# Pairing the attention chunks of a fused attention and mixture-of-experts kernel on one Trainium2 core

## The chip, the cores and the metric

The kernel runs on one core of one Trainium2 chip. The metric is the device time of one execution in microseconds (us); the value compared is the median of several runs. Five engines work side by side: TensorE (PE in the profile, its weight loads PEld), VectorE (DVE), ScalarE (ACT), GpSimd (POOL) and SyncE (SP), whose queue issues most of the DMAs.

## The reference

```python
def _attn_ref(r, k, v, w, u):            # B, H, S, D = 4, 8, 768, 48
    for t in range(S):
        cur = np.einsum('bhd,bhe->bhde', u[None] * kt, vt)
        y[:, :, t] = np.einsum('bhd,bhde->bhe', rt, state + cur)
        state = w[None, :, :, None] * state + np.einsum('bhd,bhe->bhde', kt, vt)

def _moe_ref(x, w1, w2, w3, w_out):      # 3072 tokens, 384 -> 768 -> 384
    h = np.maximum(np.maximum(x @ w1, x @ w2), x @ w3)
    return h @ w_out

def _moe2_ref(x, w_gate, w_noise, noise, w1, w2):   # 8 experts, top 2, 384 -> 1024 -> 384
    ...
```

A linear attention with a decaying state makes the tokens x. A dense layer takes the maximum of three products and projects it back. A router then sends each token to two of eight experts and adds their weighted results.

## The kernel before

The first part (to about 395 us) handles the 3072 tokens as 8 **blocks** of 384 tokens. A block is 21 **units**: 18 dense units `u_step(b, f, j)` (one of the three products for 128 of the 768 features; in block 0 three products in full float32, later nine in the split form wH and wl) and 3 projection units `x2_step(b, j)`. A dense unit writes one of two rotating PSUM banks `u`; the unit two places later writes the same bank, so it must wait until the earlier one has been read. Of the three units of a feature group, the first is read by ACT (copy to `uw`), the second and the third by DVE (`uw` = max).

The attention is done in **chunks** of 128 tokens, three for each block, one block ahead of the dense layer; every 6 chunks the state starts afresh. For a chunk, PE makes the scores (`scores`, into the banks `sc`), which DVE masks into `A`; one slot later the values `A`·v and `Rp`·state (`ymm`, bank `y`) and the state's increment (bank `st`). DVE adds these to `x` and to the next state `St`. For chunks below `NPE` = 6, PE also makes the scaled keys and the bonus weights (`x2` bank, then ACT copies `K2` and eight `sv` pieces); later chunks load a token-major copy and let DVE do that.

The units in which PE turns to attention are written down by hand: `SLOTS` = units 2, 9 and 17 of each block; there PE makes the values of one chunk and the scores of the next, one after the other. I call this a **burst**. The rest of a chunk's preparation (`prep`) is a generator of which one instruction is issued per unit. Chunks must also be transposed (token to feature order) for the dense layer: chunks 0 to 5 and every third one after that on PE (`xtr`, three transposes at unit `XTR` = 19 for the third chunk of a block), the others by a **bounce**: SP writes `x` to DRAM, reads it back in four pieces, and DVE transposes 32 by 32 (`x_bounce`, `x_turn`, five units after the burst).

DVE's remaining time is handed out by `fill`: it has a budget `room` per unit, and spends it on converting the weights (`conv`, block 0), splitting them (`splits`, blocks 0 and 1) and the router of the block before (`rgen`). Engines take their instructions in the order in which the program issues them.

The second part (from about 395 us) runs the experts. Neither its code nor its order differs between the two versions.

Of the kernel before, what the change touches and what calls it, by code (L numbers as in the profile page):

```python
# [7 lines left out]
F32 = mybir.dt.float32  # L8
# [30 lines left out]
SLOTS = (2, 9, 17)  # L39
# [4 lines left out]
TABK = 12  # L44
# [152 lines left out]
def moe_kernel(ctx, tc, rT, kT, tm, wuT, wrow, urow, mw, wout, wgn, noise, ew1, ew2, out):  # L197
# [159 lines left out]
    def prep(g):  # L357

        r_, k_, t_, v_ = LD[g]
        a = A_[g] = Ctx()  # L360
        a.v = v_
        a.Pk = at.tile([DP, 4, 128], F32, name="Pk", bufs=2)
        a.Rp = at.tile([DP, 4, 128], F32, name="Rp", bufs=2)
        a.K2 = at.tile([128, 4 * DP + 8], F32, name="K2", bufs=2)
        a.sv = at.tile([128, DM], F32, name="sv", bufs=2)
        yield v.tensor_mul(a.Pk, k_, Tk)
        yield v.tensor_mul(a.Rp, r_, Tr)
        t1 = at.tile([128, 512], F32, name="t1", tag="t1")
        if g < NPE:

            t1 = t1[:DP].rearrange("p (a c) -> p a c", a=4)
            yield v.tensor_mul(t1, r_, k_)
            pk = bank("x2")
            for pr in range(4):
                for th in TH:
                    nc.tensor.matmul(pk[th, pr * DP:pr * DP + DP], a.Pk[:, pr, th], Dg[:DP, pr * DP:pr * DP + DP],
                                     start=True, stop=True)
            red = pk[:, 4 * DP:4 * DP + 8]
            for pr in range(4):
                for th in TH:  # L380
                    nc.tensor.matmul(red[th, 2 * pr:2 * pr + 2], t1[:, pr, th], wu[:, pr, 1:], start=True, stop=True)
            nc.scalar.activation(a.K2, pk[:, :4 * DP + 8], AF.Copy)
            if g > 3:
                yield
            yield
            for h in range(H):
                hs = slice(h * D, h * D + D)
                nc.scalar.activation(a.sv[:, hs], a.v[:, hs], AF.Copy, scale=a.K2[:, 4 * DP + h:4 * DP + h + 1])
            return
        else:  # L390
            t1 = t1[:, :DM]
            tr, tk = t_[:, :DM], t_[:, DM:DM + 4 * DP]
            red = at.tile([128, H, 1], F32, name="red")
            yield v.tensor_mul(t1.rearrange("p (a b d) -> p a b d", a=4, b=2),
                               tr.rearrange("p (a b d) -> p a b d", a=4, b=2), gap(tk))
            yield v.tensor_mul(a.K2[:, :4 * DP], tk, TAB["k"])
            yield v.tensor_mul(t1, t1, ub)
            yield v.tensor_reduce(red, hd(t1), axis=AX.X, op=OP.add)
            yield v.tensor_mul(hd(a.sv), hd(a.v), red.to_broadcast([128, H, D]))
# [1145 lines left out]
```

## Time and profile before

| | us |
|---|---|
| median of 3 runs | 854.38 (854.34 to 855.59) |
| the profiled execution | 854.07 |
| its span, first to last instruction | 852.3 |

| engine | busy, us | share of the span |
|---|---|---|
| PE | 835.5 | 98% |
| DVE | 525.1 | 62% |
| ACT | 282.1 | 33% |
| POOL | 142.6 | 17% |

The busy time of PE overlaps: consecutive matmuls are pipelined, so the distance from one start to the next, and not a matmul's own duration, is the pace. DVE's share is a mean over stages that differ.

### The profile page before, as it was taken

What the parts mean: (1) busy time and instruction counts of PE and PEld (TensorE: products, weight loads), DVE (VectorE), ACT (ScalarE), POOL (GpSimd) and SP (SyncE); (2) the same over time, 40 slices, a digit from 0 to 9 for tenths busy, and PEclk for the clock granted to TensorE, in tenths of its full rate; (3) what the DMA queues carried; (4) which work ended last, traced back from release to release, by engine and by line L of the source; (5) the groups of instructions that cost most, each with busy time, mean ns of one, the idle gap of its engine ahead of it and who ended that gap; (6) DMA issues with size and microseconds to landing.
All of it is one profiled execution on the core that took longest, in us unless ns stands there. A gap on an engine that the chain in (4) does not pass through costs nothing.

```text
span 852.3 us, 17123 instructions
## 1 busy us (share of the span) xinstructions
PE 835.5 (98%) x6672; PEld 775.5 (91%) x6672; DVE 525.1 (62%) x1389; ACT 282.1 (33%) x600; POOL 142.6 (17%) x124
## 2 busy tenths in 40 slices
PE   8999999999999999999999999999999999999995
PEld 6667999999999999999989999999999999999994
DVE  8998987768677676837546672664626446264320
ACT  6334422212221231223314552433524344243221
POOL 1000030110303030110223031220222203122121
PEclk9999999999999999999999999999999999999998
DMA  9991252635525161125129774672555726553222
GB/s 288 321 257 48 81 179 72 211 135 154 179 70 159 47 182 51 39 103 131 58 70 218 191 161 102 146 170 64 124 126 133 169 78 126 119 141 47 49 30 32
DMA packets 98957, 107.82 MB, mean 127 GB/s; under 512 B 55361, under 2 KB 81714, under 8 KB 98866
## 3 DMA queue, kind: packets, MB, share of 16 engines
q1 hardware_dynamic: 88002, 86.68, 36.5%
q0 software_dynamic: 10320, 19.10, 10.8%
q8 instruction: 54, 0.88, 0.4%
q10 hardware_dynamic: 544, 0.85, 0.4%
q14 instruction: 37, 0.30, 0.1%
HBM read 73.96 MB, written 33.01 MB: 126 GB/s over the span
## 4 chain that ended last, share of the span: by engine, by line
PE 86%; DVE 5%; issue 4%; DMA 2%; POOL 1%; ACT 1%; SPq 0%; ACTq 0%; POOLq 0%; DVEq 0%
PE b_u L619 8%; PE b_u L621 7%; PE b_u L620 7%; PE b_u L860 7%; PE b_u L859 7%; PE b_u L861 7%; PE b_u L617 3%; PE b_y L426 3%; PE b_sc L407 2%; PE b_y L431 1%; PE b_y L887 1%; PE b_y L888 1%; PE b_st L889 1%; PE b_x L887 1%; PE b_tx L889 1%
## 5 line engine op out<-in xcount | busy, mean ns | idle before, releaser
L871 DVE SCALAR_TENSOR_TENSOR ghL<-b_u,ghH 128x512 fp32r<-128x512 f32 (+5 forms) x120 | 70.0, 584 | 188.9 <-ACT ghH L870 188.8
L859 PE MATMUL b_u<-gxH,e1H 128*128 128x512 f32 (+5 forms) x384 | 132.9, 346 | 0.4 <-ACT gxH L826 0.4
L860 PE MATMUL b_u<-gxL,e1H 128*128 128x512 f32 (+5 forms) x384 | 132.1, 344 | 0.1
L861 PE MATMUL b_u<-gxH,e1L 128*128 128x512 f32 (+5 forms) x384 | 131.8, 343 | 0.0
L619 PE MATMUL b_u<-xHt,wH 128*128 128x384 f32 x378 | 130.8, 346 | 0.8 <-DVE uw L628 0.8
L621 PE MATMUL b_u<-xHt,wl 128*128 128x384 f32 x378 | 127.6, 337 | 0.0
L620 PE MATMUL b_u<-xLt,wH 128*128 128x384 f32 x378 | 127.1, 336 | 0.0
L704 POOL DMA_INDIRECT XS<-rows,ii x48 | 55.2, 1150 | 384.5 <-issue 192.3
L870 ACT ACTIVATE ghH<-b_u 128x512 fp32r<-128x512 f32 (+5 forms) x120 | 61.4, 511 | 158.1 <-PE b_u L861 152.3
L861 PEld LDWEIGHTS b_u<-gxH,e1L 128*128 128x128 f32 x384 | 72.1, 188 | 8.9
L859 PEld LDWEIGHTS b_u<-gxH,e1H 128*128 128x128 f32 x384 | 72.3, 188 | 6.8 <-ACT gxH L826 0.6
L860 PEld LDWEIGHTS b_u<-gxL,e1H 128*128 128x128 f32 x384 | 72.2, 188 | 6.2 <-DVE gxL L833 0.3
L619 PEld LDWEIGHTS b_u<-xHt,wH 128*128 128x128 f32 x378 | 71.0, 188 | 4.6 <-issue 2.9
L630 ACT ACTIVATE hHt<-uw 128x384 fp32r<-128x384 f32 x48 | 25.2, 525 | 149.9 <-DVE uw L628 146.6
L952 POOL DMA_INDIRECT out_dram<-ys,gix x34 | 53.1, 1561 | 126.8 <-ACT ys L983 106.6
L628 DVE TENSOR_TENSOR uw<-b_u,uw 128x384 f32<-128x384 f32 x96 | 53.2, 554 | 31.0 <-PE b_u L621 27.3
L620 PEld LDWEIGHTS b_u<-xLt,wH 128*128 128x128 f32 x378 | 71.4, 189 | 0.0
L621 PEld LDWEIGHTS b_u<-xHt,wl 128*128 128x128 f32 x378 | 70.8, 187 | 0.0
L952 POOL DMA_INDIRECT out_dram<-yrows,gix x20 | 30.6, 1529 | 189.6 <-ACT yrows L946 185.7
L826 ACT ACTIVATE gxH<-raw 128x512 fp32r<-128x512 f32 (+4 forms) x48 | 26.1, 543 | 79.4 <-DVE raw L825 77.1
L624 ACT ACTIVATE uw<-b_u 128x384 f32<-128x384 f32 x48 | 23.5, 489 | 42.1 <-PE b_u L621 37.2
L617 PE MATMUL b_u<-xHt,wl 128*128 128x384 f32 x96 | 32.8, 492 | 0.0
(299 smaller groups left out, 1762.9 us busy)
## 6 DMA issues: line engine op xcount, KB each, us to landing
est<-in_ew_dram SPq DMA_DIRECT2D x64, 384.0 KB, 4.1
ldt<-in_tm_dram SPq DMA_DIRECT2D x18, 416.0 KB, 5.2
raw<-XS SPq DMA_DIRECT2D x32, 192.0 KB, 4.2
wS<-in_w_dram SPq DMA_DIRECT2D x15, 384.0 KB, 7.2
ldr<-in_rT_dram SPq DMA_DIRECT2D x24, 224.0 KB, 5.6
ldk<-in_kT_dram SPq DMA_DIRECT2D x22, 224.0 KB, 5.6
out_dram<-zrow SPq DMA_DIRECT2D x8, 576.0 KB, 4.7
cols<-in_tm_dram SPq DMA_DIRECT2D x22, 192.0 KB, 6.0
```

What stands on the lines that cost most here:

```text
L617: nc.tensor.matmul(o, WF[3 * f + j][:, ks], xH[b][:, k, :], start=(k == 0), stop=(k == 2))
L619: nc.tensor.matmul(o, WH[j][:, f, ks], xH[b][:, k, :], start=(k == 0), stop=False)
L620: nc.tensor.matmul(o, WH[j][:, f, ks], xL[b][:, k, :], start=False, stop=False)
L621: nc.tensor.matmul(o, WL[3 * f + j][:, ks], xH[b][:, k, :], start=False, stop=(k == 2))
L628: v.tensor_tensor(w, o, w, op=OP.max)
L704: st = nc.gpsimd.indirect_dma_start(out=XS, out_offset=bass.IndirectOffsetOnAxis(ap=ii[:, 3 * k + j:3 * k + j + 1], axis=0), in_=rw[:, j, ...
L859: nc.tensor.matmul(u, a[:, k, fs], o.xH[:, k, :n], start=(k == 0), stop=False)
L860: nc.tensor.matmul(u, a[:, k, fs], o.xL[:, k, :n], start=False, stop=False)
L861: nc.tensor.matmul(u, b[:, k, fs], o.xH[:, k, :n], start=False, stop=(k == 2))
L870: nc.scalar.activation(hH[:, :n], u, AF.Relu)
L871: v.scalar_tensor_tensor(hL[:, :n], u, 0.0, f32(hH[:, :n]), op0=OP.max, op1=OP.subtract)
L952: st = nc.gpsimd.indirect_dma_start(out=out, out_offset=bass.IndirectOffsetOnAxis(ap=o.ix[:o.n[j], j, :], axis=0), in_=ys, in_offset=None, ...
```

## The change

- `BURSTS` replaces `SLOTS`: a table of 14 bursts in place of 21. Up to chunk 9 a burst has one chunk's values and one chunk's scores. The burst at block 2, unit 2 has the values of chunk 9 and the scores of 10 and 11; from there each has the values of two chunks and the scores of the next two. The seven pairs are 10 and 11, 12 and 13, up to 22 and 23.
- In a pair the first chunk's state increment comes first and its values after it, into the bank `x2`; DVE adds the new state at once, and the second chunk's values use it within the same burst. The second state goes into the free columns of `st`, the second scores into the banks `tx` and `u`. The masking of the first scores is deferred to the two units behind.
- Chunks 11, 17 and 23 are bounced through DRAM as well; only 8, 14 and 20 are still transposed on PE after chunk 5. `x`, `xr` and `XD` get one buffer more each, and the second chunk of a pair is turned six units after the burst.
- The keys and the bonus of chunks 3, 4 and 5 (`keys`, `bonus`, formerly inside `prep`) are made at the head of their own burst. At a burst of block 0 `fill` gets 3.0 in place of 1.7.
- `prep` is split into `prep1` (products that the scores need) and `prep2` (what the values need), and `between` fixes what is issued from one burst to the next, with the loads of later chunks in between.
- Weights 16 and 22 get buffers of the rings of the others, weights 17 and 23 a buffer that later serves as `Rp`; the splits of the last weights follow the transposes of these one by one; the turned table `tk` is made at unit 17 of block 0 (`TABK`), formerly 12.

```diff
-SLOTS = (2, 9, 17)
+BURSTS = {(0, 2): ([3], [4]), (0, 9): ([4], [5]), (0, 17): ([5], [6]), (1, 2): ([6], [7]), (1, 9): ([7], [8]),
+          (1, 17): ([8], [9]), (2, 2): ([9], [10, 11]), (2, 12): ([10, 11], [12, 13]), (3, 4): ([12, 13], [14, 15]),
...
+PLAIN = (8, 14, 20)
-TABK = 12
+TABK = 17
...
+    def burst(ys, scs):
+
+        g = ys[0]
+        if len(ys) == 1:
+            ready = []
+            if g % 3 and not bounced(g - 1):
+                ready.append(xtr(g - 1))
+            if g < NPE:
+                keys(g)
+                bonus(g)
+            ready.append(ymm(g))
+        else:
+            st = bank("st")
+            s0 = st_mm(g, st)
+            y0 = y_mm(g, bank("x2"))
+            s0()
+            y0()
+            s1 = st_mm(g + 1, st[:, 192:])
+            ready = [y_mm(g + 1, bank("y")), s1]
+        first = scores(scs[0]) if scs else []
+        if len(scs) > 1:
+            tx, u = scores(scs[1], True)
+            return ready + [u, tx], first
+        return ready + first, []
...
-        return g >= 6 and g % 3 < 2
+        return g >= 6 and g not in PLAIN
...
+            here = BURSTS.get((b, k))
+            if here:
+                drain(FEED.pop(order.pop(0)))
+                if len(here[1]) > 1 or len(here[0]) > 1:
+                    while reading[0]:
+                        next(rgen)
+                    settle()
+                ready, late = burst(*here)
+                defer.extend(late)
+            elif b < NBLK - 1 and k == XTR and not bounced(3 * b + 5):
+                ready.append(xtr(3 * b + 5))
...
+            if defer and not here:
+                defer.pop(0)()
...
-                room += 1.7 if k in SLOTS else 0.0
+                room += (3.0 if b == 0 else 1.7 if len(here[0]) < 2 else 2.5) if here else 0.0
...
+                take(agen, 2 if b > 1 and (kind or j == 0) else 1)
```

The first place is PE in block 0 around the burst at unit 2 (values of chunk 3, scores of 4). Before, the rows from the scores of chunk 3 on; `b_x` is the bank of the keys, a dense unit is three rows of `b_u`:

```order
L407 MATMUL b_sc<-Rp,Pk 64x128 x16
L376 MATMUL b_x_560<-tabs,Pk 64x112 x8
L381 MATMUL b_x_560<-wu,t_524 64x2 x8
L617 MATMUL b_u<-xHt,wl 128x384 x6
L426 MATMUL b_y<-cols,A 64x48 x16
L431 MATMUL b_y<-St_141,Rp 64x96 x8
...
L407 MATMUL b_sc<-Rp,Pk 64x128 x16
L617 MATMUL b_u<-xHt,wl 128x384 x6
L376 MATMUL b_x_714<-tabs,Pk 64x112 x8
L381 MATMUL b_x_714<-wu,t_705 64x2 x8
L617 MATMUL b_u<-xHt,wl 128x384 x15
```

The same place now:

```order
L431 MATMUL b_sc<-Rp,Pk 64x128 x16
L683 MATMUL b_u<-xHt,wl 128x384 x6
L406 MATMUL b_x_597<-tabs,Pk 64x112 x8
L411 MATMUL b_x_597<-wu,t_524 64x2 x8
L449 MATMUL b_y<-cols,A 64x48 x16
L454 MATMUL b_y<-St_141,Rp 64x96 x8
...
L431 MATMUL b_sc<-Rp,Pk 64x128 x16
L683 MATMUL b_u<-xHt,wl 128x384 x21
L573 MATMUL b_tx<-ident,x 128x128 x3
L406 MATMUL b_x_793<-tabs,Pk 64x112 x8
```

The keys of chunk 3 have moved behind the first two dense units, and those of chunk 4 from between the fourth and the fifth unit to the next burst; seven dense units now follow each other. The second place is DVE at that burst, from a weight conversion (`wst`, `wS`) to the max of the third unit (`uw`). Before:

```order
L1354 TENSOR_SCALAR wl<-wst_96 128x384
L1355 SCALAR_TENSOR_TENSOR wl<-wS_95,wl 128x384
L1355 SCALAR_TENSOR_TENSOR wl<-wst_96,wl 128x384
L453 TENSOR_TENSOR x<-b_y,sv 128x4x3x32
L464 TENSOR_TENSOR St_140<-b_st,Sw 48x4x48 x2
L413 TENSOR_TENSOR A<-b_sc,maskS 128x512 x2
L372 TENSOR_TENSOR t_705<-ldr,ldk 112x512
L628 TENSOR_TENSOR uw<-b_u,uw 128x384
```

And now:

```order
L1459 TENSOR_SCALAR wl<-wst_96 128x384
L1460 SCALAR_TENSOR_TENSOR wl<-wS_95,wl 128x384
L1460 SCALAR_TENSOR_TENSOR wl<-wst_96,wl 128x384
L1461 SCALAR_TENSOR_TENSOR wl<-wS_95,wl 128x384
L1461 SCALAR_TENSOR_TENSOR wl<-wst_96,wl 128x384
L1459 TENSOR_SCALAR wl<-wst_97 128x384
L463 TENSOR_TENSOR x<-b_y,sv 128x4x3x32
L494 TENSOR_TENSOR St_140<-b_st,Sw 48x4x48 x2
L436 TENSOR_TENSOR A<-b_sc,maskS 128x512 x2
L388 TENSOR_TENSOR t_711<-ldr,ldk 112x512
L694 TENSOR_TENSOR uw<-b_u,uw 128x384
```

Three conversions stand ahead of the chunk's `x` that stood behind the max before. The third place is PE at the burst of the pair 10 and 11 (block 2, unit 12); eight rows of the first chunk's state (L478) stand ahead of these, and `tx` and `u` alternate three times more behind them:

```order
L449 MATMUL b_x_2379<-cols,A 64x48 x16
L454 MATMUL b_x_2379<-St_140,Rp 64x96 x8
L449 MATMUL b_y<-cols,A 64x48 x16
L454 MATMUL b_y<-St_141,Rp 64x96 x8
L431 MATMUL b_sc<-Rp,Pk 64x128 x16
L431 MATMUL b_tx<-Rp,Pk 64x128 x2
L431 MATMUL b_u<-Rp,Pk 64x128 x2
```

Before, each chunk had the rows L426, L431, L439 and L407 between dense units of its own, as at the first place; now one entry and one exit serve two chunks, and `St_141` is written by DVE while this burst runs.

## Rows read from the trace of the kernel before

**Rows 1.** Busy time by stage: stretch, its length, each engine's busy us (instructions), clock, DMA.

```profile
22.00:62.00 40.00, 39.20 (x415) 26.61 (x411) 39.87 (x91) 13.00 (x42) 0.00 (x0) 1.00 1.00 298
...
132.00:395.00 263.00, 263.00 (x2559) 254.60 (x2558) 185.61 (x584) 63.58 (x146) 36.03 (x30) 1.00 0.37 115
```

**Rows 2.** Timeline of PE at chunk 10's burst: start, us, line, out<-in, shapes, count.

```profile
156.97 0.34 PE L621 MATMUL b_u<-xHt,wl 128*128 128x384 f32 x1
157.23 1.14 PE L426 MATMUL b_y<-cols,A 128*64 128x48 f32 x32
158.20 0.84 PE L431 MATMUL b_y<-St,Rp 112*64 112x96 f32 x16
158.88 0.62 PE L439 MATMUL b_st<-cols,K 128*64 128x48 f32 x16
159.42 1.10 PE L407 MATMUL b_sc<-Rp,Pk 48*64 48x128 f32 x32
160.46 0.44 PE L619 MATMUL b_u<-xHt,wH 128*128 128x384 f32 x1
160.74 0.34 PE L620 MATMUL b_u<-xLt,wH 128*128 128x384 f32 x1
160.91 0.34 PE L621 MATMUL b_u<-xHt,wl 128*128 128x384 f32 x1
```

**Rows 3.** Groups by line, PE: count, busy us, mean ns of one, idle before.

```profile
L407 PE MATMUL b_sc<-Rp,Pk 48*64 48x128 f32 x736 | 25.4, 275 | 0.8 <-DVE Rp L367 0.7
...
L439 PE MATMUL b_st<-cols,K 128*64 128x48 f32 (+1 forms) x320 | 12.4, 214 | 0.0
```

**Rows 4.** Timeline of DVE at the same burst.

```profile
159.10 0.56 DVE L450 TENSOR_TENSOR x<-b_y,sv 128x384 f32<-128x384 f32 x1
159.62 0.72 DVE L464 TENSOR_TENSOR St<-b_st,Sw 48x192 f32<-48x192 f32 x2
160.56 1.29 DVE L413 TENSOR_TENSOR A<-b_sc,maskS 128x512 f32<-128x512 f32 x2 [0.22 <-PE b_sc L407]
```

**Rows 5.** Timeline of PE at the transposes of chunk 11.

```profile
181.06 0.49 PE L506 MATMUL b_tx<-ident,x 128*128 128x128 f32 x3
181.30 0.43 PE L648 MATMUL b_st<-woH,hHt 128*128 128x400 f32 x1
181.57 0.34 PE L649 MATMUL b_st<-wol,hHt 128*128 128x400 f32 x1
```

**Rows 6.** Timeline of PE in block 0, behind chunk 3's burst.

```profile
32.80 4.14 PE L617 MATMUL b_u<-xHt,wl 128*128 128x384 f32 x12
36.86 0.99 PE L376 MATMUL b_x<-tabs,Pk 112*64 112x112 f32 x16
38.11 0.63 PE L381 MATMUL b_x<-wu,t 112*64 112x2 f32 x16 [0.26 <-DVE t L372]
38.67 6.72 PE L617 MATMUL b_u<-xHt,wl 128*128 128x384 f32 x20
```

**Rows 7.** Timeline of DVE in the same stretch.

```profile
33.77 0.36 DVE L1354 TENSOR_SCALAR wl<-wst 128x384 int32<-128x384 int32 x1
34.04 0.56 DVE L1355 SCALAR_TENSOR_TENSOR wl<-wS,wl 128x384 int32<-128x384 int32 x1
34.51 0.56 DVE L1355 SCALAR_TENSOR_TENSOR wl<-wst,wl 128x384 int32<-128x384 int32 x1
34.98 0.56 DVE L453 TENSOR_TENSOR x<-b_y,sv 128x384 f32<-128x384 f32 x1
...
37.98 0.55 DVE L628 TENSOR_TENSOR uw<-b_u,uw 128x384 f32<-128x384 f32 x1
...
41.32 0.55 DVE L628 TENSOR_TENSOR uw<-b_u,uw 128x384 f32<-128x384 f32 x1
...
45.13 0.68 DVE L366 TENSOR_TENSOR Pk<-ldk,T 112x512 f32<-112x512 f32 x1
45.73 1.02 DVE L1356 SCALAR_TENSOR_TENSOR wl<-wS,wl 128x384 int32<-128x384 int32 x2
```

**Rows 8.** Timelines of DVE and of PE in block 1, behind chunk 7's burst.

```profile
109.56 0.56 DVE L556 TENSOR_TENSOR wl<-wl,wH 128x384 fp32r<-128x384 f32 x1 [1.00 <-ACT wH L555]
...
116.18 0.44 PE L619 MATMUL b_u<-xHt,wH 128*128 128x384 f32 x1 [0.56 <-DVE uw L628]
```

**Rows 9.** PE's first and last matmuls; a stretch near the end, as rows 1.

```profile
2.40 3.84 PE L304 MATMUL b_tx<-wz 128*128 128x512 bf16 x11 [2.40 <-POOL wz L298]
...
841.50 0.34 PE L972 MATMUL b_st<-e2H,e1L 128*128 128x384 f32 x1
...
844.00:845.00 1.00, 0.00 (x0) 0.00 (x0) 0.00 (x0) 0.00 (x0) 0.28 (x1) 0.87 0.32 25
```

**Rows 10.** The bounce's DMAs (tile XD, all writes and reads), us from issue to landing.

```profile
DMA to landing us min/median/max: 1.7/1.9/3.6
```

More of the change, by code (lines that the diff above doesn't have):

```diff
@@ L364, in prep, with prep2 @@
+    def prep2(g):
+        l, a = LD[g], A_[g]
+        a.v = l.v
         a.K2 = at.tile([128, 4 * DP + 8], F32, name="K2", bufs=2)
         a.sv = at.tile([128, DM], F32, name="sv", bufs=2)
-        yield v.tensor_mul(a.Pk, k_, Tk)
-        yield v.tensor_mul(a.Rp, r_, Tr)
         t1 = at.tile([128, 512], F32, name="t1", tag="t1")
         if g < NPE:
[L371 to L388, printed above, removed]
-            return
-        else:
[L391 to L399, printed above, removed]
@@ new lines, in prep2, with keys @@
+        yield v.tensor_mul(a.K2[:, :4 * DP], tk, TAB["k"])
+        yield v.tensor_mul(t1, t1, ub)
+        yield v.tensor_reduce(red, hd(t1), axis=AX.X, op=OP.add)
+        yield v.tensor_mul(hd(a.sv), hd(a.v), red.to_broadcast([128, H, D]))
+    def keys(g):
+        a = A_[g]
+        pk = bank("x2")
+        for pr in range(4):
+            for th in TH:
+                nc.tensor.matmul(pk[th, pr * DP:pr * DP + DP], a.Pk[:, pr, th], Dg[:DP, pr * DP:pr * DP + DP],
+                                 start=True, stop=True)
+        red = pk[:, 4 * DP:4 * DP + 8]
+        for pr in range(4):
+            for th in TH:
+                nc.tensor.matmul(red[th, 2 * pr:2 * pr + 2], a.t1[:, pr, th], wu[:, pr, 1:], start=True, stop=True)
+        nc.scalar.activation(a.K2, pk[:, :4 * DP + 8], AF.Copy)
@@ L404, in scores, with bonus @@
+    def bonus(g):
+        a = A_[g]
+        for h in range(H):
+            hs = slice(h * D, h * D + D)
+            nc.scalar.activation(a.sv[:, hs], a.v[:, hs], AF.Copy, scale=a.K2[:, 4 * DP + h:4 * DP + h + 1])
+    def scores(g, second=False):
+        a = A_[g]
+        if second:
+            sc = [bank("tx"), bank("u", 2)]
+        else:
+            sc = [bank("u" if g == 1 else "sc", 2) for _ in range(2)]
         for pr in range(4):
@@ L1001, in take @@
             next(gen, None)
-    pg = [prep(g) for g in range(4)]
-    take(pg[0], 3)
+    p1 = [prep1(g) for g in range(4)]
+    p2 = [prep2(g) for g in range(4)]
+    drain(p1[0])
+    drain(p2[0])
     s0 = scores(0)
@@ L1012, in moe_kernel @@
     load_next[0] = NWST
-    take(pg[1], 2)
-    s0()
-    take(pg[0], 2)
+    drain(p1[1])
+    evacs(s0)
+    keys(0)
+    bonus(0)
     s1 = scores(1)
-    take(pg[1], 1)
+    drain(p2[1])
     y0 = ymm(0)
-    s1()
-    take(pg[2], 2)
-    y0()
-    take(pg[2], 1)
-    drain(pg[1])
+    evacs(s1)
+    drain(p1[2])
+    y0()
+    drain(p2[2])
+    keys(1)
+    bonus(1)
     s2 = scores(2)
@@ L1027, in moe_kernel @@
     x0()
-    s2()
+    evacs(s2)
     take(conv, 2)
-    take(pg[2], 1)
+    keys(2)
     y1 = ymm(1)
-    drain(pg[2])
+    bonus(2)
     take(conv, 2)
@@ L1051, in moe_kernel @@
     unit = [0]
-    ahead = None
     room = 0.0
+    defer = []
+    FEED = dict(between())
+    order = list(BURSTS)
     def splits_may(k):
-        return 24 if k > 16 else min(len(WGT) + 2, 6) if WGT else 0
+        return 24 if k > 16 else len(WGT) + 1 if WGT else 0
     def fill(b, k):
@@ L1142, in moe_kernel @@
             waiting += evs
-            if b < NBLK - 1:
-                next(agen, None)
-                if k >= XTR and g + 2 < NCH:
-                    ahead = ahead or prep(g + 2)
-                    next(ahead, None)
+            if order:
+                agen = FEED[order[0]]
+                take(agen, 2 if b > 1 and (kind or j == 0) else 1)
             if b == 0:
```

195 lines of the change are left out of this document (115 added, 80 removed), and 2 rows, old and new, of the table BURSTS.

## The prediction

> **What bounds the kernel now.** I first read the busy time by stage [rows 1]. From 132 to 395 us PE is busy 263 of 263 us at full granted clock, while DVE works 185.61 and ACT 63.58 us: there PE alone sets the end, and what leaves PE leaves the total. In block 0 (22 to 62 us) there are two limits: PE is busy 39.20 and DVE 39.87 of 40 us, because the weight conversions fill every hole that DVE has. An edit there must be asked twice: what it does to PE, and what it puts ahead of DVE's urgent work.
>
> Then I read PE's timeline by distances between starts. At chunk 10's burst [rows 2] the last dense matmul starts at 156.97 and the first of the values at 157.23, where the next dense one would have started .17 later (160.74 to 160.91): the entry costs .09. At the end, dense matmuls start at 160.46 and 160.74: the exit costs .28 - .17 = .11. The burst between takes 3.23.
>
> The sum below is made against the profiled execution, 854.07 us; the median of the three runs, 854.38, is .31 above it, and I add that at the end. A measurement of this kernel can tell about 0.2%, 1.7 us, from no change.
>
> **The pairs (chunks 10 to 23, seven bursts for fourteen).** The matmuls stay; entries, exits and the switches inside change. From [rows 2], in a single burst the values' first half takes .97, the second (state) half .68, the state's increment .54, the scores 1.04: 3.23. The last two include a switch. A chunk's 32 scores span 1.10 to the end of the last, whose own duration is .275 [rows 3], so 31 intervals take .825, and scores followed by scores need .85. In the same way the 16 increments have 15 intervals in .62 - .214 = .406 [rows 2, 3], .43 for all; .54 minus .43 is the switch from increments to scores, .11. A pair is then: increments .45 (with a small switch), values .97 + .68, increments .45, values .97 + .68 + .10 (switch to scores), scores .85 + 1.04, which is 6.19 against two times 3.23 = 6.46. That is .27 less; one entry and one exit saved are .09 + .11 = .20. Together .47 a pair, times 7: **-3.3**. The trace has no step from increments to values, nor back: two such in each pair, 14 in all, cost nothing at least and at most the .11 of increments to scores each, so the bounds are about -3.4 and -2.0. I take the near end, since the matmuls on both sides have the same shape, 128x64 by 128x48.
>
> The second chunk's values need the state that DVE adds during the burst. From the end of the first increments, the first chunk's values (1.65) and the second's first half and increments (.45 + .97 or so) give DVE about 3 us; its two additions took .72 at chunk 10's burst [rows 4], and even behind a whole second instruction of that length they are in time. I cost it at nothing. The scores in bank `u` must be masked before the unit after next: the unit in between takes 9 x .175 = 1.58, a mask half of the 1.29 of two [rows 4], .65, so .9 is left. At nothing too; this is the thinnest cover, and it is the slower rival below.
>
> **Transposes of chunks 11, 17, 23.** Each took .24 and raised the distance behind the next matmul to .27 [rows 5], where .175 is usual: .24 + .095 = .34, three times: **-1.0**. What replaces them is a write and reads through DRAM, with 1.9 us from issue to landing in the median and 3.6 at most [rows 10]. Two bounces in turn make four landings, 7.6 us; behind the second `x` PE still has the scores (1.9) and six units (9.5), 11.4 us, before DVE turns the second chunk. Hidden. Only at 3.6 for each (14.4) would DVE wait some 3 us, and PE behind it.
>
> **Block 1.** After chunk 7's burst a split on DVE waited 1.00 for ACT's `wH`, and PE waited .56 for the `uw` behind it [rows 8]. With its wH-part issued elsewhere this split lies earlier, and the stall has no cause left: with the start of the next matmul **-.7** (bounds 0 and -.7).
>
> **Block 0: keys of 3 to 5, and 3.0 in place of 1.7.** This is the part that can lose. The unit two places later writes the same bank, so the fifth dense unit waits for `uw` of the third, which DVE started at 37.98 and ended at 38.53 [rows 7]. Before, that wait was hidden: PE did two units from 32.80, then the keys from 36.86 and, after .26 for DVE's `t`, from 38.11, and began the fifth unit at 38.67 [rows 6], .14 behind DVE. Now the keys of chunk 4 are gone from there, and PE is ready at about 36.8. At the same time DVE has three more conversions ahead of `x`: two `SCALAR_TENSOR_TENSOR`, whose starts are .47 apart (34.51 - 34.04), and one `TENSOR_SCALAR`, .27 (34.04 - 33.77) [rows 7]: 1.21. `uw` then runs from 39.19 to 39.74, and PE starts at about 39.8: a wait of **+3.0**. The next such maximum stood 3.34 later (41.32); ahead of it DVE now also has chunk 5's `Pk` and `Rp`, which take .60 each (45.73 - 45.13 for `Pk` [rows 7]). So it would end at 39.74 + 3.34 + 1.20 = 44.3; PE has two units of twelve matmuls in 4.06 (32.80 to 36.86 [rows 6], .1 of it an exit), 3.9, and is ready at 43.7: **+.65**. The burst at unit 9 has the same three conversions; its DVE is less far behind, +.5 (0 to 1). On the other side the keys of 4 and 5 lose their own entries and exits, .2 each, and the wait of .26: **-.66**. Block 0 in sum: **+3.5**. The lower end is less: conversions brought forward leave holes later on, so that the second and third wait may vanish and a part of the first (2.2 in sum); the upper end adds .5 for the second wait and .5 for the third, about 4.5. Taken: 3.5, because DVE in this stretch has .13 us free in 40 [rows 1], so that whatever stands in front of `uw` delays it in full.
>
> The other edits (the rings of weights 16, 17, 22, 23, `TABK` at 17, the split of `prep`, the loads between bursts) move work of ACT, SP and DVE between units that PE fills with no idle time; ahead of 62 us they move DVE's work within its own total. I cost them at nothing; uncovered, each would be one DVE instruction of about .5 late, once per block at most. The experts are unchanged and only start earlier or later.
>
> **The sum.** -3.3 - 1.0 - .7 + 3.5 = -1.5: 852.6 for the profiled execution, **852.9** for the median.
>
> **The rivals.**
>
> *The clock falls during the wait.* [...] At the end of the kernel the last matmul starts at 841.50 and is over at 841.84, and the stretch from 844 to 845 has a granted clock of .87 [rows 9]: if the lower level is half, it came in .26 of that microsecond, near 844.74, 2.9 us after PE had stopped. My wait is 3.0 long. The price is that of a start: 11 warm-up matmuls took 3.84 us [rows 9] where 11 x 512/384 x .175 = 2.57 are due, 1.3 more. 852.9 + 1.3 = 854.2. [...]
>
> *The waits of block 0 are smaller.* The conversions brought forward have to be made in block 0 in any case, and made earlier they leave later holes; if DVE is ahead by the length of them at the fifth unit, `uw` is not late. Half of the three waits (4.15) gives 852.9 - 2.1 = 850.8, none 848.7. Against it: [rows 7] show starts without a hole, .14 ahead of PE's.
>
> *Merging saves nearly nothing.* If the new steps between increments and values, and scores that alternate between two banks, cost what entry and exit did, the pairs give 1 instead of 3.3: about 855.
>
> *Slower: DVE is late with the second scores.* In a pair DVE has a second `x`, a state sum and 2.5 of fill between the burst and the masking of bank `u`; the unit after the next one waits for it. Cover is .9. From the point where DVE comes 1.3 us late in each of the eight bursts with two chunks' scores or values, PE waits .4 there, 3.2 in all, and the saving of the pairs is gone; at 1.5 late it is .6 each, 4.8, and the time 857.7. For it: it is the one place where DVE's order gates PE in every block. Against it: DVE works 185.61 of 263 us there [rows 1], so it is free three tenths of the time.
>
> **How the numbers follow.** The sum as it stands .38; the clock .22; smaller waits .17; little from merging .11; late masking .12. The likeliest is the sum, 852.9. The range of 8 in 10 takes in the clock (854.2) and little merging (855), on the low side half of the block-0 loss gone with the rest at its best end (850.4), on the high side a mild form of the late masking (856.2). Faster by over 1.7 us means below 852.67: the smaller waits in full (.17) and about .4 of the sum's own .38, whose bounds from pairs, block 1 and block 0 are over 1 us to each side (.15): **.32**. Slower means above 856.1: the late masking, **.12**. The rest, **.56**, is within 0.2%.
>
> **What would show it.** In block 0, near 37 to 40 us, a PE wait of about 3.0 on DVE's `uw` at the fifth dense unit, one of about .65 two units later, and the granted clock from 37 to 45 us, which decides the clock rival. The pair bursts should be about 6.2 us long from entry to exit (the two at a fresh state shorter), with steps of under .05 from increments to values. No transposes of chunks 11, 17, 23 on PE, and no wait of DVE at their turned reads. No wait at chunk 7's burst. No PE wait on the mask of `u` in blocks 2 to 7. The prediction is wrong if the block-0 waits are below 1 us or above 5, or if PE idles anywhere from 132 to 395 us.

## The result and the profile after

The changed kernel takes 865.65 us (865.28 to 867.61, 4 runs) where the kernel before takes 854.41: a ratio of 1.0132 (95% interval 1.012 to 1.0144), 11.2 us slower. The forecast was 852.9, with a range from 850.4 to 856.2. The profiled execution is the longest of the four, 867.61, with a span of 865.7; PE's start-up was late in it (below), which the three others need not share.

The busy time by stage, to be read beside [rows 1] (stretch, its length, each engine's busy us, clock, DMA share):

```profile
22.00:62.00 40.00, 36.54 (x430) 25.30 (x428) 38.67 (x88) 12.79 (x40) 0.00 (x0) 0.95 0.91 290
40.00:42.00 2.00, 0.00 (x0) 0.00 (x0) 1.97 (x5) 0.00 (x0) 0.00 (x0) 1.00 0.97 292
...
44.00:46.00 2.00, 2.00 (x5) 1.09 (x4) 2.00 (x5) 0.00 (x0) 0.00 (x0) 0.50 0.05 20
84.00:90.00 6.00, 6.00 (x113) 5.45 (x110) 1.83 (x4) 3.66 (x12) 0.00 (x0) 0.72 0.00 0
132.00:395.00 263.00, 260.26 (x2621) 252.10 (x2621) 186.64 (x567) 61.71 (x146) 31.52 (x31) 1.00 0.39 125
```

From 40 to 42 us PE does nothing, from 44 to 46 its granted clock is .50, and from 84 to 90 it is .72 on the mean. PE's rows are named by the lines of the changed kernel: L683 is a dense unit of block 0 and L685 to L687 one of a later block, L406 and L411 the keys, L449 and L454 the two halves of the values, L478 the increments, L431 the scores, L573 the transposes of `x`, L357 the turn of the table. What PE waited for, after its start (instruction, what ended the wait; us in sum, times, longest):

```profile
PE b_u L683 <- DVE uw L694: 3.4, 3, 2.9
PE b_x L406 <- DVE wol L669: 2.5, 1, 2.5
...
PE b_u L685 <- DVE uw L694: 2.3, 6, 0.5
PE b_tx L357 <- DVE xLt L580: 1.5, 1, 1.5
PE b_y L454 <- DVE St L494: 1.0, 1, 1.0
```

The third and the last of these rows are in blocks 1 to 7, the others in block 0. From 132 to 395 us PE is busy 260.26 of 263, so it idles there 2.74, which the prediction named as a sign that it is wrong. I measure block 0 from the first dense matmul to the first one in block 1 that uses `wl`. Before (PE's timeline):

```profile
25.50 0.59 PE L617 MATMUL b_u<-xHt,wl 128*128 128x384 f32 x1
...
90.40 0.34 PE L621 MATMUL b_u<-xHt,wl 128*128 128x384 f32 x1
```

After, with the places where PE stood:

```profile
27.26 4.14 PE L683 MATMUL b_u<-xHt,wl 128*128 128x384 f32 x12
...
35.78 4.14 PE L683 MATMUL b_u<-xHt,wl 128*128 128x384 f32 x12
42.86 7.45 PE L683 MATMUL b_u<-xHt,wl 128*128 128x384 f32 x17 [2.94 <-DVE uw L694]
...
83.66 1.12 PE L406 MATMUL b_x<-tabs,Pk 112*64 112x112 f32 x16 [2.51 <-DVE wol L669]
84.51 1.03 PE L411 MATMUL b_x<-wu,t 112*64 112x2 f32 x16
85.33 1.99 PE L449 MATMUL b_y<-cols,A 128*64 128x48 f32 x32
...
89.25 2.20 PE L683 MATMUL b_u<-xHt,wf 128*128 128x384 f32 x6
92.94 0.57 PE L357 MATMUL b_tx<-ident,tk 112*128 112x112 f32 x4 [1.50 <-DVE xLt L580]
...
103.86 0.34 PE L687 MATMUL b_u<-xHt,wl 128*128 128x384 f32 x1
```

Block 0 was 64.90 and is 76.60. Of these 11.7, about 1.3 are the keys of chunk 3, which stood ahead of the first unit before (24.17 to 25.50), so block 0 itself lost 10.4 where I forecast 3.5. The matmuls of the fifth unit and of chunk 5's burst show the clock: 32 matmuls of the values take 1.99 at 85.33, where such a row takes 1.14 in [rows 2]; the granted clock is .69 from 84 to 85 us, .50 from 85 to 87 and .61 from 87 to 88.

Blocks 1 to 7, from that matmul to the last of its kind, took 319.19 before (90.40 to 409.59) and 319.53 after (103.86 to 423.39), where I forecast 5 less. What is left of the 13.4 between the spans is the start, less .4 by which the rest of the kernel is shorter (442.3 for 442.7): the first unit starts 1.76 later although the keys have left. PE's clock stood at half from 16 to 22 us in this execution (.53, .50 and .50 in three stretches of 2 us); in the two later profiles of the same program that unit starts at 25.50 and 25.62.

The first pair's burst (chunks 10 and 11), on PE and on DVE:

```profile
177.28 0.61 PE L478 MATMUL b_st<-cols,K 128*64 128x48 f32 x15
177.68 0.25 PE L449 MATMUL b_x<-cols,A 128*64 128x48 f32 x1
...
179.31 1.16 PE L449 MATMUL b_y<-cols,A 128*64 128x48 f32 x32
181.47 0.88 PE L454 MATMUL b_y<-St,Rp 112*64 112x96 f32 x16 [1.00 <-DVE St L494]
```

```profile
178.49 0.55 DVE L694 TENSOR_TENSOR uw<-b_u,uw 128x384 f32<-128x384 f32 x1
180.69 0.72 DVE L494 TENSOR_TENSOR St<-b_st,Sw 48x192 f32<-48x192 f32 x2 [1.65 <-ACT Sw L484]
```

ACT at the same place:

```profile
179.07 0.52 ACT L696 ACTIVATE hHt<-uw 128x384 fp32r<-128x384 f32 x1 [4.27 <-DVE uw L694]
179.50 1.16 ACT L484 ACTIVATE Sw<-St,w 112x96 f32<-112x96 f32 x4
```

The step from increments to values (177.68, .40 behind 177.28 and so 15 intervals of .027) costs nothing, as taken. But the state came late: DVE's `St` waited for `Sw`, the old state times its decay, which ACT makes behind a copy of the `uw` that DVE ended at 179.04.

### The profile page after: what moved, and what is told of

Read it like the earlier page. It is cut to its first block, busy times and chain, and to the rows that moved or that the text cites. A ratio compares the mean times of both kernels' runs of the same rounds, so it can differ in the third digit from the quotient of the medians.

```text
span 865.7 us, 17130 instructions
## 1 busy us (share of the span) xinstructions
PE 839.7 (97%) x6663; PEld 779.0 (90%) x6663; DVE 527.9 (61%) x1392; ACT 282.7 (33%) x600; POOL 137.3 (16%) x124
## 3 DMA queue, kind: packets, MB, share of 16 engines
q0 software_dynamic: 10320, 19.10, 10.4%
## 4 chain that ended last, share of the span: by engine, by line
PE 75%; DVE 12%; issue 5%; DMA 3%; ACT 2%; POOL 1%; SPq 0%; ACTq 0%; POOLq 0%; DVEq 0%
PE b_u L930 7%; PE b_u L929 7%; PE b_u L931 7%; PE b_u L685 6%; PE b_u L686 5%; PE b_u L687 5%; PE b_u L683 2%; DVE uw L694 1%; DVE A L436 1%; DMA ldk<-in_kT_dram 1%; PE b_y L449 1%; PE b_y L957 1%; PE b_y L958 1%; PE b_st L959 1%; PE b_x L957 1%
## 5 line engine op out<-in xcount | busy, mean ns | idle before, releaser
L685 PE MATMUL b_u<-xHt,wH 128*128 128x384 f32 x378 | 130.7, 346 | 2.4 <-DVE uw L694 2.3
L687 PE MATMUL b_u<-xHt,wl 128*128 128x384 f32 x378 | 127.5, 337 | 0.0
L774 POOL DMA_INDIRECT XS<-rows,ii x48 | 50.0, 1042 | 403.5 <-issue 200.0
L685 PEld LDWEIGHTS b_u<-xHt,wH 128*128 128x128 f32 x378 | 71.0, 188 | 7.4 <-DVE uw L694 5.2
L687 PEld LDWEIGHTS b_u<-xHt,wl 128*128 128x128 f32 x378 | 70.8, 187 | 0.0
L683 PE MATMUL b_u<-xHt,wl 128*128 128x384 f32 x102 | 36.7, 511 | 3.4 <-DVE uw L694 3.4
L683 PEld LDWEIGHTS b_u<-xHt,wl 128*128 128x128 f32 x102 | 19.4, 197 | 17.8 <-DVE uw L694 5.3
```

What stands on the lines that cost most here:

```text
L683: nc.tensor.matmul(o, WF[3 * f + j][:, ks], xH[b][:, k, :], start=(k == 0), stop=(k == 2))
L685: nc.tensor.matmul(o, WH[j][:, f, ks], xH[b][:, k, :], start=(k == 0), stop=False)
L687: nc.tensor.matmul(o, WL[3 * f + j][:, ks], xH[b][:, k, :], start=False, stop=(k == 2))
L774: st = nc.gpsimd.indirect_dma_start(out=XS, out_offset=bass.IndirectOffsetOnAxis(ap=ii[:, 3 * k + j:3 * k + j + 1], axis=0), in_=rw[:, j, ...
```

## The experiments

Each kernel ran beside the kernel before (855.2 to 856.0 in all of them). The chip differs from one measurement to the next, and the unaltered changed kernel, run twice more on one of them, took 880.62 and 882.2, not 865.65. So kernels of different measurements are compared by stretches of their profiles, not by totals. Block 0 of the unaltered kernel, which was 76.6, was 76.3 and 76.8 in these two; "block 0" is always this stretch. Where the profile can't name what ended a wait, it says "issue" (no signal that it shows ended it) or "remote" (a signal whose sender it can't tell).

**room17.**

```diff
-                room += (3.0 if b == 0 else 1.7 if len(here[0]) < 2 else 2.5) if here else 0.0
+                room += (1.7 if b == 0 else 1.7 if len(here[0]) < 2 else 2.5) if here else 0.0
```

> Only the 3.0 of fill at the bursts of block 0 goes back to 1.7. Theory (three conversions ahead of x and uw are a part of the wait at the fifth unit): that wait falls from 2.9 by 1.2 to about 1.7, PE's clock no longer falls behind it (about 1.6 gained), 865.65 - 2.8 = 862.8. Rival (fill only moves work, and DVE is late for another reason): the wait stays near 2.9 and the time at 865.6.

878.76, ratio 1.0287 (1.0267 to 1.0307). PE at the fifth unit:

```profile
36.12 1.13 PE L683 MATMUL b_u<-xHt,wl 128*128 128x384 f32 x3
39.00 4.14 PE L683 MATMUL b_u<-xHt,wl 128*128 128x384 f32 x12 [1.74 <-DVE uw L694]
```

The wait fell from 2.94 to 1.74, by the 1.2 of three conversions, and the 12 matmuls behind it take 4.14, as at 27.26 in the first profile, where the clock is 1.00 (27 to 31 us). The unit after the next begins 4.55 later (43.55) in place of 5.67 (48.53 - 42.86): of the 1.7 that the low clock had cost, 1.1 come back, since that unit, now earlier, waits .41 for `uw`. So far the theory holds. But the wait ahead of chunk 5's keys grew from 2.5 to 3.2: block 0 is 74.8, some 1.5 less, not 2.8.

**keys_between.**

```diff
-        items = [(prep2, g) for g in ys if g > 3]
+        items = []
+            for g in ys:
+                items += [(prep2, g)] * (g > 3) + [(keys, g), (bonus, g)] * (3 < g < NPE)
...
-            if g < NPE:
+            if g == 3:
                 keys(g)
```

> The keys and the bonus of chunks 4 and 5 stand between the dense units again, those of chunk 3 stay in the burst. Theory (the keys were PE's cover for DVE's late uw, and at unit 17 the keys of chunk 5 wait for a bank that the router's logits hold): the wait at the fifth unit falls from 3.4 to about 1.8, the one of 2.5 ahead of chunk 5's keys is gone, and both falls of the clock (1.6 and 1.3) with them: 865.65 - 1.6 - 2.8 - 2.9 + .4 for two more entries and exits = 858.7. Rival (DVE is late in any case and the waits only move on): 863 or more.

874.83 (1.0232, 1.0215 to 1.025). PE after chunk 3's burst:

```profile
37.39 0.99 PE L406 MATMUL b_x<-tabs,Pk 112*64 112x112 f32 x16
39.94 0.63 PE L411 MATMUL b_x<-wu,t 112*64 112x2 f32 x16 [1.56 <-DVE t L388]
40.50 2.20 PE L683 MATMUL b_u<-xHt,wl 128*128 128x384 f32 x6
43.72 3.49 PE L683 MATMUL b_u<-xHt,wl 128*128 128x384 f32 x10 [1.01 <-ACT uw L690]
```

With the cover back, PE waits for DVE's `t` (1.56, before .26 [rows 6]), since the conversions still stand ahead of it, and then for ACT, which here got keys and bonus in one go. Chunk 5's keys no longer wait; the table's turn does, 2.8 in place of 1.2 to 1.5. Block 0 is 73.5: 2.8 less, where I expected over 6. The cover alone does not do it, and the rival holds for the most part.

**keys5_st.**

```diff
-        pk = bank("x2")
+        pk = bank("st" if g == 5 else "x2")
```

> The keys of chunk 5 go into the bank st, which is free there, in place of x2. Theory (they wait for the router's logits in x2, which DVE reads behind splits that wait for ACT): the wait of 2.5 at unit 17 is gone and the fall of the clock behind it (1.3), 865.65 - 3.8 = 861.8. Rival (DVE's and ACT's lateness holds up whatever stands next, the table's turn first): PE waits some 2.5 longer there, 865.

878.38 (1.0271, 1.0241 to 1.0301). The keys start right behind the transposes and take .99, as in [rows 6] at a clock of 1.00 (1.12 in the first profile), so the shared bank was the wait. Part of it returns at the table's turn, which waits 2.6:

```profile
81.58 0.55 PE L573 MATMUL b_tx<-ident,x 128*128 128x128 f32 x3
82.06 0.99 PE L406 MATMUL b_st<-tabs,Pk 112*64 112x112 f32 x16
...
90.88 0.57 PE L357 MATMUL b_tx<-ident,tk 112*128 112x112 f32 x4 [2.60 <-DVE xLt L580]
```

Block 0 is 73.6, 2.7 less, where 3.8 were expected.

**singles.** One burst a chunk from chunk 10, third chunks turned on PE, loads as before.

```diff
-BURSTS = {(0, 2): ([3], [4]), (0, 9): ([4], [5]), (0, 17): ([5], [6]), (1, 2): ([6], [7]), (1, 9): ([7], [8]),
...
+BURSTS = {(b, SLOTS[j]): ([3 * b + 3 + j], [3 * b + 4 + j] if b < 6 or j < 2 else []) for b in range(7) for j in range(3)}
-PLAIN = (8, 14, 20)
+PLAIN = (8, 11, 14, 17, 20, 23)
```

> Block 0 as changed, but from chunk 10 on one burst for each chunk again (units 2, 9, 17), and chunks 11, 17 and 23 turned on PE as before. Theory (from block 1 on the pairs and the turns save PE 3.6 by the distances of starts, and new waits of 4.1 in place of one of .7 take it back): 865.65 + 3.6 - 3.4 = 865.9, with waits under 1 in blocks 1 to 7. Rival A (the pairs cost on the whole): 862 or less. Rival B (the pairs save what was forecast, 4.3, and the loss is all in block 0): 869.5 or more.

866.85 (1.0136, 1.0119 to 1.0153). That is about the changed kernel's first result, and near the 865.9 of the theory, but some 14 less than the changed kernel took later. Block 0 is 77.6, as lost as ever; blocks 1 to 7 take 320.65 (319.19 before), mainly because five bursts at unit 17, at whose start the scatter is just ending, are .3 to .4 longer, with short waits named issue in three of them. On this same chip the three kernels above, with their pairs, took 332.2 to 332.6 in blocks 1 to 7; the first pair's burst alone took 13.7 to 14.2 in them, where the first profile has 6.9.

**changed_again** (no edit).

> The changed kernel itself, unaltered, beside the next three. In room17, keys_between and keys5_st PE waited for its own instructions in the first pair's burst, some 8 us, and in the changed kernel's profile it did not, with the same instructions on PE and the scatter's DMAs at the same place. If that stall hangs on the order of DVE's and ACT's work, this run has none and the time is 865.6 as before; if it comes and goes with the run's surroundings, it can stand here too, and the time is 874 to 878.

880.62 (1.0298, 1.0281 to 1.0315). Block 0 is 76.3 again, but blocks 1 to 7 take 335.2 in place of 319.5. The same burst as above:

```profile
177.22 1.11 PE L449 MATMUL b_y<-cols,A 128*64 128x48 f32 x25
178.76 0.33 PE L449 MATMUL b_y<-cols,A 128*64 128x48 f32 x3 [0.43 <-issue]
179.51 0.29 PE L449 MATMUL b_y<-cols,A 128*64 128x48 f32 x3 [0.42 <-issue]
...
182.42 0.48 PE L454 MATMUL b_y<-St,Rp 112*64 112x96 f32 x3 [1.04 <-issue]
```

PE runs one to five matmuls at a time and waits for nothing that the profile shows ("issue"), until its pace falls too: the 32 scores that begin at 185.88 take 1.98, where such a row takes 1.10 in [rows 2]. In room17, where PE halts in the same way, the granted clock is .50 from 180 to 189 us. The burst lasts 14.3 in place of 6.9, and from its first matmul to block 3's first unit it is 35.0 in place of 26.3.

**block0_old.** Room 1.7, keys as in keys_between, those of 3 ahead of the first unit, `TABK` 12.

> Block 0 as before the change (room 1.7, keys of 3 ahead of the first unit, of 4 and 5 between units, table turned at unit 12), pairs and turns from chunk 10 as changed. Theory (the loss lies in block 0): without stalls for instructions 865.65 - 11 = about 854.5, since the 3.6 that the pairs save go into waits; with the stalls about 863. Rival (block 0's order is a small part): over 866.

874.73 (1.0222, 1.0204 to 1.0241), 5.9 under the changed kernel beside it. Block 0 is 67.1; PE's start was 3.5 late here, with a granted clock of .72 from 16 to 18 us and .50 from 18 to 22, as in the first profile (.53 and .50). The edits together give 9.2, less 1.3 for chunk 3's keys, 7.9: more than each gave by itself, but not the whole loss.

**clock.**

```diff
+WAITS = {(0, 4): 12, (0, 17): 10}
...
+            if (b, k) in WAITS:
+                warm(WAITS[b, k])
             here = BURSTS.get((b, k))
```

> 12 idle matmuls (128x512 of zeros) ahead of the fifth unit of block 0 and 10 ahead of the burst at unit 17, in the time in which PE waits there; all other work as in the changed kernel. Theory (PE's clock falls because PE stands still for 2.5 to 3 us, and costs 1.6 and 1.3 on top of the waits): the waits end where they did, the granted clock stays at 1.00 behind them, and the time is 2.9 below the changed kernel's on the same chip. Rival (the clock falls whatever PE does there, or the idle matmuls delay the real ones): no gain, or up to 3 slower.

879.7 against 880.62 (1.0287, 1.027 to 1.0304, of before). From 43 to 44 us, in `clock` and then in the unaltered kernel:

```profile
43.00:44.00 1.00, 1.00 (x5) 0.60 (x4) 1.00 (x3) 0.00 (x0) 0.00 (x0) 1.00 0.12 38
```

```profile
43.00:44.00 1.00, 1.00 (x2) 0.42 (x2) 1.00 (x3) 0.00 (x0) 0.00 (x0) 0.50 0.00 0
```

With idle matmuls in the wait the clock stays at 1.00 there, and from 84 to 86 us, at the burst at unit 17, it is 1.00 as well, where the unaltered kernel has .50. So at these two places standing still was what lowered it. The fifth and sixth units take 4.55 in place of 5.66. But the time is only .9 less, where 2.9 was expected: the next wait (the table's turn) takes what was won, 2.6 in place of 1.2.

**scatter_late.**

```diff
+SCATTERS = {2: 15, 4: 13, 6: 13}
...
-        while 0 < b < NBLK - 2 and unit[0] < SCATTER:
+        while 0 < b < NBLK - 2 and unit[0] < SCATTERS.get(b + 1, SCATTER):
```

> As changed, but the scatter of the routed rows is started at unit 15 of block 2 and 13 of blocks 4 and 6, behind the pair's burst there, in place of 11. Theory (PE's instructions are fetched beside the scatter's small DMAs, and a pair's burst of matmuls of 27 ns uses them up too fast): no wait of PE for instructions in the bursts at units 12 and 10; where the unaltered kernel has the stall on this chip it is gone (866), where it has not the time is the same within 1. Rival (the fetch is late for another reason): the stall stands as in the unaltered kernel.

870.77 (1.0184, 1.0167 to 1.0201): 9.9 under the unaltered kernel beside it. Blocks 1 to 7 take 323.0 in place of 335.2, 12.2 less; block 0 came out 1.4 longer (77.7). The first pair's burst has no wait named issue and lasts 6.75. What is left of such waits lies in the bursts at unit 17 of blocks 3 and 5, 7.5 each, in which the scatter that starts at unit 11 is not yet over:

```profile
PE b_x L450 <- issue: 1.6, 4, 0.5
```

**pairs_b0.** Block 0 with PE's order of before, pairs, and the scatter of scatter_late; the bonus at a unit of its own:

```diff
+                items += [(prep2, g)] * (g > 3) + [(keys, g), (bonus, g), (None, 0), (None, 0)] * (3 < g < NPE)
```

> Block 0 with PE's order exactly as before the change (the keys and the bonus of 4 and 5 at units of their own too), the pairs and turns as changed, and the scatter behind the pairs' bursts (15, 13, 13). Theory (the loss of 11.2 is block 0's waits, and the 15 more on another chip are PE's waits for instructions beside the scatter): block 0 takes 65 from its first unit to block 1, as before, in place of 76; blocks 1 to 7 save 3.6 and wait some 4 to 5: 855.3 + 1 = 856, within 2. Rival (the pairs themselves cost): 860 or more.

860.45 (1.0067, 1.0054 to 1.0081), where 856 within 2 was expected. The first unit of block 1 is at 91.87, against 90.40 before: block 0's loss is gone. Blocks 1 to 7 take 324.0, 4.8 over before. Of these, 2.7 are the bursts at unit 17 of blocks 3 and 5 (7.5 each where a pair without such waits takes 6.17), 1.1 is a wait of the scores of chunk 7 for DVE's `Rp`, and some .8 a wait for ACT's `hHt`. So the time is the rival's, but by these waits, and the pairs still gain nothing.

**best.** As pairs_b0, with `0.9 if len(here[0]) < 2 else 1.4` of fill from block 1 and `Sw` made between bursts.

> As pairs_b0, and from block 1 on fill gets 0.9 in place of 1.7 at a single burst and 1.4 in place of 2.5 at a pair's, and the decayed state Sw of a pair's first chunk is made between the bursts. Theory (the waits of .4 to .7 behind five bursts come from fill's router work ahead of x and uw, the one of 1.0 in the first pair's burst from Sw behind a copy on ACT): these waits, 3.9 in sum, are gone, and 3.6 are saved: 855.3 - 3 = 852 to 853, faster than before the change. Rival (DVE is late for its order, not for fill, or the router's work comes late elsewhere): as pairs_b0.

865.18 (1.0117, 1.0101 to 1.0132): worse than the rival, which had the time of pairs_b0. With less fill the router and its scatter come later: the one of block 0 now meets the burst at unit 17 of block 1, with waits named issue there (5.5 in place of 3.2), the bursts at unit 17 of blocks 3 and 5 take 10.2 and 8.5 in place of 7.5, and two waits for `uw` grew to 1.1.

**block0_exact and changed_third.** The first is pairs_b0 with the scatter at 11, the second the changed kernel.

> Block 0 as before the change (as in pairs_b0), everything from block 1 on as changed, the scatter at unit 11 too. Theory (block 0 costs 10 to 11 wherever the kernel runs, the stalls for instructions at the pairs' bursts 0 or some 14): block 0 takes 65 to 66 from its first unit to block 1 in place of 76, and the time is 10.5 below that of the changed kernel beside it: 855 where the bursts run without stalls, 870 where they stall. Rival (what is saved in block 0 comes back behind it, as a later burst then meets the scatter worse): under 6 below it.

> The changed kernel unaltered, once more, beside block0_exact. If the stalls at the pairs' bursts belong to this program on every chip but the first, 880; if they come and go between chips, anything from 865 to 881, with all of the difference between blocks 2 and 6 and none in block 0.

873.54 (1.0199, 1.0158 to 1.024) and 882.2 (1.0302, 1.0281 to 1.0315): 8.7 apart, on one chip, where 10.5 was expected. Block 1 begins 10.3 earlier; blocks 1 to 7 take 337.4 and 336.0, so 1.4 of it is lost again there. The first matmul of block 1 that uses `wl`, in block0_exact and in changed_third:

```profile
92.17 0.34 PE L684 MATMUL b_u<-xHt,wl 128*128 128x384 f32 x1
```

```profile
102.46 0.34 PE L687 MATMUL b_u<-xHt,wl 128*128 128x384 f32 x1
```

**singles_scatter8.**

```diff
-SCATTER = 11
+SCATTER = 8
```

> As singles (one burst a chunk, block 0 as changed), with the scatter started at unit 8, so that its six DMAs lie beside the whole of the burst at unit 9 in blocks 2 to 6, in place of between two bursts. Theory (PE runs out of instructions where many short matmuls in a row meet the scatter's DMAs, whatever makes the row): waits named issue in these bursts, each at least .4, and the time over that of singles (866.85) by 2 to 15. Rival (only a burst of twice the length uses up what PE has at hand): no such waits and 867 within 1.

896.03 (1.0485, 1.0469 to 1.0501): 29 over singles (866.85, on another chip). The burst itself runs through (3.22), so the waits expected in it did not come; PE and ACT stop behind it. The last of the six scatters on POOL, ACT, and then PE in block 2; the last row is PE in block 3:

```profile
176.66 1.17 POOL L772 DMA_INDIRECT XS<-rows,ii  x1 [0.30 <-issue]
178.12 0.49 ACT L688 ACTIVATE uw<-b_u 128x384 f32<-128x384 f32 x1 [9.06 <-remote]
```

```profile
178.66 0.69 PE L683 MATMUL b_u<-xHt,wH 128*128 128x384 f32 x1 [4.17 <-issue]
...
233.17 0.69 PE L683 MATMUL b_u<-xHt,wH 128*128 128x384 f32 x1 [4.97 <-ACT uw L688]
```

ACT resumed .3 after the last of the six scatters ended (176.66 + 1.17 = 177.83). PE's unit waits for ACT to read its bank, as the row of block 3 says. ACT in turn waits for a signal: the 30 waits of this copy in which the profile names PE's last matmul of the unit as the sender (23.7 us in sum) make PE the likely one behind "remote" too. The copy began at 178.12, 5.55 behind the start of the last matmul of the unit it copies (172.57), which takes .34. So I take it that PE's matmuls, or their signal, were late, and not ACT's instructions. Such stops of PE, of 1.5 to 5 us, stand in each of blocks 2 to 6. So a pair is not needed. Nor is a burst beside the scatter always enough: in the first profile of the changed kernel the scatter ran from 178.75 to 186.10, beside the whole of the first pair's burst, without such a wait.

**pairs_clear.** As pairs_b0, the scatter at unit 8 in blocks 3 and 5 too, `Sw` early, .9 of fill at single bursts from block 1.

> As pairs_b0, with the scatter at unit 8 of blocks 3 and 5 too (ahead of the pair's burst at unit 17, whose start it overlapped), Sw of a pair's first chunk made between the bursts, and .9 of fill in place of 1.7 at the bursts with one chunk's values from block 1 on. Theory (each of these removes a wait seen in pairs_b0: for instructions 2.2 with the clock behind it, 1.0 for the state, .6 and .7 at two bursts): 860.45 - 5 = 855.5, level with the kernel before. Rival (the waits come back elsewhere, as in best): 859 or more.

858.22 (1.0032, 1.002 to 1.0044), .3% over before, between the theory's 855.5 and the rival's 859. With `Sw` made early the first pair's burst has no wait for the state, and lasts 5.71 in place of 6.91; with the scatter moved, the bursts at unit 17 of blocks 3 and 5 last 6.17. Some of what is left of PE's waits in blocks 1 to 7:

```profile
PE b_u L689 <- DVE uw L698: 1.6, 4, 0.6
...
PE b_st L487 <- issue: 1.0, 3, 0.4
...
PE b_x L718 <- ACT hHt L700: 0.7, 1, 0.7
```

Blocks 1 to 7 take 321.4, 2.6 less than in pairs_b0 and still 2.2 over before. The middle row stands in the burst at unit 17 of block 1, as in best. So the rival holds in part: some of the waits came back elsewhere, and no version here beats the kernel before.

## Why the prediction was wrong

The profiled spans differ by +13.4 where I forecast -1.5, 14.9 apart: 6.9 of it in block 0 (10.4 for 3.5), 5.3 in blocks 1 to 7 (+.3 for -5), 3.1 at the start of this execution (1.76, and the 1.3 of the keys that have left), less the .4 of the rest. Two steps of the prediction failed, both of them terms put at nothing: the waits of the moved work at its new place in block 0, and DVE's and ACT's lateness in blocks 1 to 7.

**The sizes of the pairs and turns were right.** By PE's timeline, read as in [rows 2], the 14 bursts from chunk 10's on sum to 41.4 us before; after, the seven pairs' sum to 38.6 without the wait of 1.2 in the first, and the burst ahead, which now has a second chunk's scores, takes 4.10 in place of 3.22: 39.5; seven entries and exits at .20 are 1.4. Together 3.3, the -3.3 of the sum. (Its far bound, -3.4, is -3.6 by its own rows, where steps that cost nothing also save the .02 in each increment of .45.) A full pair lasts 6.17 from entry to exit (6.19 forecast), and the steps from increments to values are free. The nine transposes that are gone, three for each of the three chunks, gave 1.1 (1.0 forecast). The stall behind chunk 7's burst is gone too, as forecast, but one of .43 now stands behind chunk 6's.

**Waits took it back; "at nothing" was the failed step.** Blocks 1 to 7 became .3 longer instead of 5 shorter. PE waits 2.3 for `uw` at six units, .2 of it in block 7 as before, and 1.0 for `St`. By the distances of starts, with the restart of the matmuls behind them, the new waits for `uw` cost 4.3 and the one for `St` 1.2, together 5.5, where before there was one of .8, now gone. That is 4.7 more against the 4.4 saved, which is the .3. I had held DVE's free three tenths and a cover of 3 us for the state against them; what decided was the queue: ACT's `Sw` behind a copy that waits for DVE, and masks, later chunks' products, transposes and the router's work on DVE ahead of `uw`. The late-masking rival was near in size, 3.2 to 4.8, but not in place: no wait of PE is on a mask.

**Block 0: the first term was right, the list was not complete.** The wait at the fifth unit was 2.94 (+3.0 forecast). The second (+.65) did not come in this profile, where PE's clock was .50 from 44 to 46 us; in `clock`, at 1.00, and in room17 it was .41. Those after unit 9 were .2 and .27 (+.5 forecast). The clock rival was right as a mechanism: 1.7 (fifth unit 3.50, sixth 2.17, against 2.04 and 1.94 before) where I priced 1.3, and `clock` shows the cause. The lower level is half, as the rival took it: .50 here, and .50 from 845 to 846 us in the kernel before, behind the .87 of [rows 9]. The second fall came behind a wait of 2.51, which I had thought short enough to escape it ("Against it"). But two waits ahead of the table's turn, 2.60 in keys5_st and 2.59 in `clock`, were followed by matmuls at starts .18 apart, as in the first profile at a clock of 1.00 (93 to 96 us), so the length of the wait alone does not tell.

What I did not have is what the moved work itself waits for at its new place. The keys of chunk 5 went from unit 10 to 17. There their bank holds the products that fold the router's weights into `w_out` (the expectations call them the router's logits) until DVE has read them, and DVE reads them (L669) behind splits that wait for ACT:

```profile
79.01 1.91 DVE L622 TENSOR_TENSOR wol<-wol,woH 128x384 fp32r<-128x384 f32 x3 [2.58 <-ACT woH L621]
...
82.94 0.58 DVE L669 TENSOR_TENSOR wol<-b_x,woH 128x16 fp32r<-128x16 f32 x6
```

That is a wait of 2.51, and 1.6 of low clock in that burst. And `TABK` at 17, which stood among the edits costed at nothing, put a matmul behind DVE's `xLt`: 1.50. I asked of the keys only what PE loses where they left. 2.94 + 1.7 + .5 + 2.5 + 1.6 + 1.5 less .66 for entries and exits is 10.1 of the 10.4.

These terms are not independent: each taken away alone gave 1.2 to 2.8 in block 0, always less than expected of it (2.8 to over 6), since a large part of what PE gains it next spends waiting for a DVE that is as late as before. Together they gave 7.9 (block0_old) and 9.7 (block0_exact against changed_third), without chunk 3's keys. That block 0 is the cause of the first result is shown by block0_exact (8.7 on one chip, with block 1 beginning 10.3 earlier) and by the first profile itself, in which blocks 1 to 7 differ by .3.

**What was not in the prediction at all** is the scatter. Before, it began behind the burst at unit 9 and ran for 9 us, into the first 1.7 us of the burst at unit 17, without a wait of PE; a pair's burst at unit 10 or 12 lies beside it whole. In the first measurement this cost nothing; in the two later ones of the same program blocks 1 to 7 took 335.2 and 336.0 against 319.5, some 16 more. Scatter_late takes 12.2 of it back, and singles_scatter8 brings 29 without any pair, so on these chips the place of the scatter decides. How it holds PE up is not shown. That PE lacks instructions, which the expectations assume, was argued from the word "issue" and from the resuming with the scatter's end; no run shows it. The profile has a DMA queue that it names "instruction"; whose instructions it carries is not shown. The queues of changed_again from 176 to 186 (packets, MB, share of 16 engines):

```profile
q0 software_dynamic: 384, 1.21, 32.7%
q1 hardware_dynamic: 928, 0.79, 27.2%
q8 instruction: 1, 0.02, 0.9%
```

One packet of .02 MB in 10 us does not explain three matmuls each .7 us, and the first profile, which has no stall, has one of .02 MB as well from 177 to 187 us. So these queues do not show that the stall came with late instructions. Why the first measurement was spared (its record does not name the chip) and which part of the scatter does it stay open.

## What to carry to other kernels

When work is moved, ask three things of its new place: which bank or buffer it shares there and who must first read it, what stands ahead on the engine that will read it, and which DMAs run beside it; what it leaves uncovered at the old place is only the first half. On an engine that alternates between full and waiting, take the sum of waits away together or not at all: one alone returns at the next. And before explaining a slow experiment, run the unaltered kernel beside it.

## What the runs showed of the hardware

The same program took 865.65 once and 880.62 and 882.2 later, with the kernel before within 1.6 us beside it. Waits of PE of 2.94 and of 2.51 were each followed by a clock of .50 (44 to 46 and 85 to 87 us); matmuls on zeros in these waits, twelve in the first and ten in the second, kept it at 1.00 (41 to 47 and 82 to 86 us in `clock`). Waits of 2.60 (keys5_st) and 2.59 (`clock`) ahead of the table's turn were not: the matmuls behind them start .18 apart. In start-up, from 18 to 22 us, the clock was .50 in the first profile, keys5_st and block0_old, in which PE had been idle for .63, 1.05 and .96 us from 14 to 18, but 1.00 in changed_again and changed_third, with .78 and .96 there.
